# k and q in two loads of 48 rows, gates contiguous, constants in two tiles, and one activation table asked for first

## The chip, the cores and the metric

The kernel runs on one NeuronCore of a Trainium2 chip. The metric is the device time of one execution in microseconds. Three runs of the kernel before gave 475.73, 475.87 and 477.15 us; the median is 475.87 us.

The core has five engines that run side by side, each working off its own row of instructions in order: TensorE (PE; the loads of its stationary operand are shown apart as PEld), VectorE (DVE), ScalarE (ACT), GpSimd (POOL) and SyncE (SP), which here issues nearly all DMAs. An instruction starts when its engine is free and the semaphores that it waits for have been raised.

## The reference

Two batches of eight heads go through a gated recurrence over 768 time steps with head size 40 (mLSTM); the result, 1536 tokens of 320 values, goes through two gated feed-forward layers of width 1536.

```python
for t in range(S):                       # S = 768
    m_new = np.maximum(f_gate[:, :, t] + m, i_gate[:, :, t])
    f_stab = np.exp(f_gate[:, :, t] + m - m_new)
    i_stab = np.exp(i_gate[:, :, t] - m_new)
    m = m_new
    C = f_stab[:, :, None, None] * C + i_stab[:, :, None, None] * np.einsum('bhd,bhe->bhde', vt, kt)
    n = f_stab[:, :, None] * n + i_stab[:, :, None] * kt
    h_tilde = np.einsum('bhde,bhe->bhd', C, qt)
    nq = np.einsum('bhd,bhd->bh', n, qt)[:, :, None]
    y[:, :, t] = o * h_tilde / np.maximum(np.abs(nq), 1.0)     # o = sigmoid(o_gate)

x = (sigmoid(x @ w_gate) * (x @ w_val)) @ w_out                # layer 1
x = ((x @ w_a) * (x @ w_b)) @ w_out2                           # layer 2
```

Everything but the six feed-forward weights is float32; the weights arrive as float64.

## The kernel before

The recurrence is computed in 12 steps of 64 time steps each. In step s the decay between two time steps comes out of the gates: a matmul E (two of them, for even and odd heads, `ph_E`, line 366, into a tile e) makes the exponents out of the tiles lhsE and rhsE, and ScalarE exponentiates them (X, `ph_exp`, line 373, into Dt). The products of k and q are S (`ph_S`, lines 396 and 411, out of the tile kq). VectorE multiplies S by Dt (P, line 421, into Z), and k by a column of Dt (Kw, line 376). TensorE then makes the step's output O (line 440) and the state for the next step, ST (line 430), which ScalarE copies back into the tile Y (line 452). The feed-forward units (lines 519 to 528) follow as tokens become ready, and take most of the time. Two tiles are used alternately for e (two banks), Dt and Z, three for kq and Y.

The weights come as pairs of 32-bit words; ScalarE and VectorE turn each block into float32 (lines 213 to 237) and split it (lines 247 to 258). The gates are loaded in three chunks of 128, 320 and 320 time steps; their running maximum and sums are `gate_parts` (lines 276 to 307).

A constant tile cs holds, side by side, an identity matrix (for transposes, and as a stationary operand in S), the patterns for rhsE and lhsE, a small identity for Y (`y_init`, line 569) and two columns of signs for the gates.

The order of each engine's instructions is that of the written list PLAN. A task stands there by name: E10 is the matmul E of step 0, odd heads (E, then the half, then the step), X00 its exponential, kq0 a load, na0 the first conversion of weight block 0, ge1 the gate step on ScalarE. A number behind a star, as in `E00*37`, puts that many dummy matmuls on a zeroed tile in front (line 169, tile first). A DMA waits for what its destination needs and, since eight semaphores are used in turn, for the eighth DMA before it.

The kernel's first activation (line 193) writes two elements that are overwritten later; it is there for its activation table. A table has to be loaded before a function that the present one lacks; copy and absolute value need none.

Of the kernel before, what the change touches and what calls it, by code (L numbers as in the profile page):

```python
# [7 lines left out]
F32 = mybir.dt.float32  # L8
# [43 lines left out]
NH = 4 * P + DM  # L52
E1 = D + 1

C_ID = 0
C_RE = C_ID + P
C_LD = C_RE + 512
C_IP = C_LD + 2 * P
C_AB = C_IP + D
C_N = C_AB + 2  # L60


EXP_LO = 2.0**-15
# [1 line left out]


PLAN = """
start gl1 cst rhs0:A lhs0:A ga0 ga1 gb0 gd0 ge0 lhs1:A w0 gb1 na0 gc0 gd1 ge1 pr0:V E00*37 og0 X00 rhs1:A
pr1:V nb0 yz0 kv0 E01*1 E10*6 gl2 gc1 yz2 ns0 yz1 kv1 X01 X10 ga2 pr2:V yi0:A nc0 k10:V kq0 yi2:A k00:V E11*4
X11 S0 pr3:V w1 kq1 E02 kq2 nd0:V E12 P10 P00 yi1:A k01:G kv2 ST0 st0 na1 X02 og2 S1*10 X12 k11:G k12:G og1  # L70
kq3 gb2 gd2 O0 kv3 ST1 P11 P01 S2*2 pr4:V sg0 nb1 E03 s10 N0 O1*2 P02 P12 st1 s30:G k02:G kq4 ST2 sg2 N1 s20:V
# [59 lines left out]
def kernel(  # L131
    ctx: ExitStack,
    tc: tile.TileContext,
    gates: bass.AP,
    cst: bass.AP,
    kqT: bass.AP,
    kv: bass.AP,
    ogate: bass.AP,
# [4 lines left out]
    nc = tc.nc  # L143
# [34 lines left out]


    cs = xpool.tile([P, C_N], F32, tag="cs", name="cs")  # L180
    ident = cs[:, C_ID : C_ID + P]

    x2tok = xpool.tile([P, NSTEP, 3 * P], F32, tag="x2tok", name="x2tok")

# [5 lines left out]

    Y = [apool.tile([P, 2, NPAIR, B, E1 + D], F32, tag=f"Y{i}", name=f"Y{i}") for i in range(3)]
    Z = [apool.tile([P, 2, NPAIR, B, T], F32, tag=f"Z{i}", name=f"Z{i}") for i in range(2)]
    nc.scalar.activation(Z[0][:, 0, 0, 0, 0:2], zb[:, 0:2], AF.Sigmoid)
    Kw = [apool.tile([P, 2, NPAIR, B, D], F32, tag=f"Kw{i}", name=f"Kw{i}") for i in range(2)]
    PR = ((slice(64, 128), slice(0, 64)), (slice(0, 64), slice(64, 128)))

# [67 lines left out]
    def load_gates(i):  # L264

        c0, n = GCH[i]
        w = wpool.tile([P, 2 * NH + 2 * P], F32, tag=f"W{NWB - 1 - i}", name=f"gates{i}")[0:64]
        g = w[:, 0 : 2 * n].rearrange("p (x t) -> p x t", x=2)
        gws[i] = g, w[:, 2 * n : 3 * n], w[:, 3 * n : 4 * n], w[:, 4 * n : 5 * n + 1]
        nc.sync.dma_start(g, gates[:, :, c0 : c0 + n])  # L270

    def gate_parts(i):
        c0, n = GCH[i]
        s0 = 0 if i else 1

        def part0():
            g, lf, L, ms = gws[i]
            if i == 0:
                nc.vector.memset(ms[:, 0:1], -1e30)
                nc.vector.memset(lf[:, 0:1], 0.0)  # L280
            else:
                nc.vector.tensor_copy(ms[:, 0:1], mlast[0])
            nc.vector.tensor_tensor_scan(ms[:, 1:], g[:, 1], g[:, 0], ms[:, 0:1], op0=ALU.add, op1=ALU.max)
            mlast[0] = ms[:, n : n + 1]
            nc.vector.tensor_tensor(lf[:, s0:], g[:, 1, s0:], ms[:, s0:n], op=ALU.add)

        def part1():
            g, lf, L, ms = gws[i]
            nc.vector.tensor_tensor(lf[:, s0:], lf[:, s0:], ms[:, s0 + 1 :], op=ALU.subtract)
            nc.vector.tensor_tensor(g[32:64, 0], g[32:64, 0], ms[32:64, 1:], op=ALU.subtract)  # L290

        def part2():
            g, lf, L, ms = gws[i]
            nc.vector.tensor_tensor_scan(L, rm[:, 0:n], lf, 0.0, op0=ALU.mult, op1=ALU.add)
            nc.vector.tensor_tensor(L[32:64], g[32:64, 0], L[32:64], op=ALU.subtract)

        def part3():
            g, lf, L, ms = gws[i]
            hi = g[:, 1].bitcast(F32R)
            nc.scalar.activation(hi, L, AF.Copy)  # L300
            nc.scalar.activation(lf, hi.bitcast(F32), AF.Copy, scale=cs[0:64, C_AB + 1 : C_AB + 2])

        def part4():
            g, lf, L, ms = gws[i]
            nc.vector.scalar_tensor_tensor(
                V[:, c0 : c0 + n], L, cs[0:64, C_AB : C_AB + 1], lf, op0=ALU.mult, op1=ALU.subtract
            )

        return part0, part1, part2, part3, part4


# [78 lines left out]
    def ph_S(s):  # L390
        if s < NQ:

            sp = [ps_tile("acc", f"sp{par}_{s}") for par in range(2)]
            for par in range(2):
                _, qr = PR[par]
                nc.tensor.matmul(
                    sp[par][qr],
                    cs[qr.start : qr.start + D, C_ID + qr.start : C_ID + qr.stop],
                    kq[s][qr.start : qr.start + D, 1].rearrange("p a b t -> p (a b t)"),
                    start=True, stop=True,  # L400
                )
# [98 lines left out]
    def ph_T(s):  # L500
        Tps[s] = transp(ps_tile("e", f"tp{s}"), xtok[s])
# [61 lines left out]
    def y_init(i, e):  # L563
        for par in range(2):
            _, qr = PR[par]
            y = Y[i][qr, par, :, :, E1:].rearrange("p a b d -> p (a b) d")
            x = cs[qr, C_IP : C_IP + D].unsqueeze(1).to_broadcast([64, NPAIR * B, D])
            if e is None:
                nc.scalar.activation(y, x, AF.Copy)
            else:  # L570
                e.tensor_copy(y, x)
# [99 lines left out]

    task("start", "D", lambda: load_gates(0))
    task("cst", "D", lambda: nc.sync.dma_start(cs, cst))

    def t_copy(e, out, x):
        if e is None:
# [12 lines left out]
        task(f"lhs{i}", "AG", lambda e, i=i: t_lhs(i, e), ("cst",))  # L689
    for i in range(3):  # L690
        task(f"yz{i}", "G", lambda i=i: nc.gpsimd.memset(Y[i].rearrange("p x a b e -> p (x a b e)"), 0.0))
        task(f"yi{i}", "AG", lambda e, i=i: y_init(i, e), ("cst", f"yz{i}"))
    for i in range(len(OGS)):
        task(f"og{i}", "D", lambda i=i: load_og(i))
        task(f"sg{i}", "A", lambda i=i: ph_sig(i), (f"og{i}",))
# [2 lines left out]
    for i, (c0, n) in enumerate(GCH):  # L698
        if i:
            task(f"gl{i}", "D", lambda i=i: load_gates(i))  # L700
        a, b, c, c2, c3 = gate_parts(i)
        task(f"ga{i}", "V", a, [f"gl{i}" if i else "start"] + ([f"ga{i-1}"] if i else []))
        task(f"gb{i}", "V", b, [f"ga{i}"])
        task(f"gd{i}", "V", c, [f"gb{i}"])
        task(f"ge{i}", "A", c2, [f"gd{i}", "cst"])
        task(f"gc{i}", "V", c3, [f"ge{i}"])
    for i in range(NPREP // 2, NSTEP // 2):
        s = 2 * i
# [4 lines left out]
    for s in range(NSTEP):  # L713
# [16 lines left out]
                task(f"q{p}{n}", "VG", lambda e, s=s, p=p: ph_qg(s, p, e), ["kq" + n, f"X{p}{n}"] + back("O", 2))  # L730
            task(f"k{p}{n}", "VG", lambda e, s=s, p=p: ph_kw(s, p, e), ["kv" + n, f"yi{s % 3}", f"X{p}{n}"] + back("ST", 2))
        if s < NQ:
            task("S" + n, "P", lambda s=s: ph_S(s), ["kq" + n, "cst"], [("acc", [f"P{p}{n}"]) for p in range(2)])
        else:
            task("S" + n, "P", lambda s=s: ph_S(s), ["kq" + n], [("e", ["P0" + n, "P1" + n])])
        o_in = [z + n for z in zs] + ["kv" + n, f"yi{s % 3}"] + back("st", 1)
# [95 lines left out]
    assert len(done) == len(tasks)  # L832


_INS = ["gates", "cst", "kqT", "kv", "ogate", "w1", "w2"]


def _layout(inputs):
# [15 lines left out]
    def rows(g):  # L854
        return g[rb, 2 * rpair + rpar]

    a["gates"] = np.stack([rows(ig), rows(fg)], 1)

    def tr(z):

        z = z.reshape(B, NPAIR, 2, NSTEP, T, D).transpose(2, 5, 3, 1, 0, 4)
        o = np.zeros((P, NSTEP, NPAIR * B * T), dt)
        o[:D], o[64 : 64 + D] = z.reshape(2, D, NSTEP, NPAIR * B * T)
        return o.transpose(1, 0, 2)

    a["kqT"] = np.concatenate([tr(k), tr(q)], 2)
# [38 lines left out]
    for par in range(2):  # L905
# [5 lines left out]
    c[0:D, C_IP : C_AB] = np.eye(D)
    c[64 : 64 + D, C_IP : C_AB] = np.eye(D)
    lo = rlo == 1
    c[0:64, C_AB] = lo
    c[0:64, C_AB + 1] = np.where(lo, 1.0, -1.0)
# [23 lines left out]
```

## Time and profile before

| | |
|---|---|
| median of three runs | 475.87 us |
| the profiled execution | 475.26 us |
| its span, from the first to the last instruction | 473.4 us |
| TensorE busy | 463.8 us (98%) |
| VectorE busy | 295.5 us (62%) |
| ScalarE busy | 242.7 us (51%) |
| GpSimd busy | 102.5 us (22%) |
| moved by DMA | 39.31 MB, 83 GB/s over the span |

Busy time is the time in which an instruction of the engine runs. Matmuls overlap and their ends are modelled, so that a busy TensorE is not TensorE at its peak. The time stands for the whole run; single stages have other limits, so they are read in windows of time. Times in rows count from the start of the span. In a row of a timeline the first number is the start, the second the duration, and the bracket says how long the engine had stood idle before, and what, by the profile, ended that. The granted clock (PEclk) is 1.00 where TensorE's records show no throttling.

### The profile page before, as it was taken

How to read it: one execution, taken by the hardware profiler on the slowest of the kernel's cores; microseconds unless marked ns; L12 is line 12 of the kernel's file. 1: busy time of each engine (PE TensorE's matmuls, PEld its weight loads, DVE VectorE, ACT ScalarE, POOL GpSimd, SP SyncE). 2: the span in 40 equal slices, each digit the busy share in tenths (PEclk: the TensorE clock that was granted, in tenths of full speed). 3: DMA queues.
4: the chain of work that ended last, by engine and by line, in shares of the span. 5: the costliest groups of instructions: out<-in, count | busy, mean ns of one | idle time of the engine just before them, and what ended most of it. 6: DMA issues, size and time to landing. Idle time of an engine off the chain costs nothing.

```text
span 473.4 us, 8681 instructions
## 1 busy us (share of the span) xinstructions
PE 463.8 (98%) x3516; PEld 404.1 (85%) x3516; DVE 295.5 (62%) x505; ACT 242.7 (51%) x455; POOL 102.5 (22%) x110
## 2 busy tenths in 40 slices
PE   9899999999999999999999999999999999999995
PEld 3478989999998889888888898888989888888885
DVE  7989998998655663637675564565655727524243
ACT  5999978668672635343464432645452415322130
POOL 3234327613340014100320311103140003200000
PEclk9899999999999999999999999999999999999998
DMA  7968454243022040300202120024021020001121
GB/s 239 335 203 281 150 162 114 60 147 114 1 83 84 1 168 12 131 25 1 83 1 83 66 102 1 6 86 160 10 80 77 1 84 1 0 1 26 31 55 55
DMA packets 10454, 39.31 MB, mean 83 GB/s; under 512 B 1840, under 2 KB 3760, under 8 KB 10416
## 3 DMA queue, kind: packets, MB, share of 16 engines
q1 hardware_dynamic: 10128, 38.45, 25.0%
q8 instruction: 27, 0.44, 0.4%
q10 hardware_dynamic: 288, 0.33, 0.2%
q14 instruction: 11, 0.09, 0.1%
HBM read 36.71 MB, written 1.97 MB: 82 GB/s over the span
## 4 chain that ended last, share of the span: by engine, by line
PE 86%; DVE 6%; DMA 3%; ACT 2%; issue 1%; POOL 1%; DVEq 0%; POOLq 0%
PE pa L519 30%; PE pb L519 23%; PE acc L526 8%; PE acc L527 8%; PE acc L528 8%; PE o L440 2%; DMA Y<-in_kv_dram 2%; DMA kq<-in_kqT_dram 2%; PE sp L411 2%; PE st L430 1%; PE first L169 1%; PE t L482 1%; DVE g L551 1%; PE tp L482 1%; PE e L366 1%; DVE Z L421 1%
## 5 line engine op out<-in xcount | busy, mean ns | idle before, releaser
L519 PE MATMUL pa<-xb,W 128*128 128x512 f32 (+1 forms) x864 | 169.7, 344 | 0.2 <-DVE ge L600 0.2
L519 PEld LDWEIGHTS pa<-xb,W 128*128 128x128 f32 x864 | 136.4, 188 | 19.1 <-DVE ge L600 0.6
L519 PE MATMUL pb<-xb,W 128*128 128x512 f32 x480 | 119.0, 392 | 0.0
L519 PEld LDWEIGHTS pb<-xb,W 128*128 128x128 f32 x480 | 89.0, 188 | 17.9
L555 ACT ACTIVATE gh<-g 128x512 fp32r<-128x512 f32 (+1 forms) x84 | 47.5, 568 | 110.5 <-PE acc L527 55.6
L526 PE MATMUL acc<-W,gh 128*128 128x320 f32 x288 | 89.3, 310 | 0.0
L527 PE MATMUL acc<-W,gh 128*128 128x320 f32 x288 | 88.9, 309 | 0.0
L528 PE MATMUL acc<-W,gl 128*128 128x320 f32 x288 | 88.8, 308 | 0.0
L549 DVE TENSOR_TENSOR g<-g,pb 128x512 f32<-128x512 f32 x60 | 40.9, 685 | 69.7 <-PE pb L519 61.7
L560 DVE TENSOR_TENSOR gl<-g,gh 128x512 fp32r<-128x512 f32 (+1 forms) x66 | 45.5, 694 | 44.0 <-ACT gh L555 43.9
L544 ACT ACTIVATE g<-pa 128x512 f32<-128x512 f32 x60 | 35.6, 595 | 45.8 <-DVE gl L560 38.1
L527 PEld LDWEIGHTS acc<-W,gh 128*128 128x128 f32 x288 | 54.0, 188 | 2.1
L526 PEld LDWEIGHTS acc<-W,gh 128*128 128x128 f32 x288 | 54.0, 188 | 2.0
L528 PEld LDWEIGHTS acc<-W,gl 128*128 128x128 f32 x288 | 54.0, 188 | 0.0
L253 POOL TENSOR_TENSOR W<-wst,W 128x832 fp32r<-128x832 f32 x9 | 19.1, 2123 | 84.5 <-DVE x2tok L634 42.2
L634 DVE SCALAR_TENSOR_TENSOR x2tok<-acc,x2tok 128x320 f32<-128x320 f32 x52 | 23.8, 484 | 19.5 <-PE acc L528 19.5
L237 POOL TENSOR_TENSOR wst<-cva,wst 128x960 int32<-128x960 int32 x7 | 16.9, 2411 | 73.9 <-DVE cva L231 61.1
L213 ACT ACTIVATE cva<-wst 128x960 f32<-128x960 f32 x24 | 25.8, 1075 | 10.4 <-DVE wst L237 8.8
L247 ACT ACTIVATE W<-wst 128x832 fp32r<-128x832 f32 x24 | 23.1, 965 | 12.0 <-DVE wst L237 9.0
L231 DVE SCALAR_TENSOR_TENSOR cva<-wst,cva 128x960 int32<-128x960 int32 x24 | 27.9, 1160 | 0.4
L560 POOL TENSOR_TENSOR gl<-g,gh 128x256 fp32r<-128x256 f32 x18 | 15.7, 877 | 54.6 <-ACT gh L555 44.9
L214 ACT ACTIVATE wst<-wst 128x960 int32<-128x960 uint32 x24 | 25.9, 1080 | 0.0
(85 smaller groups left out, 473.1 us busy)
## 6 DMA issues: line engine op xcount, KB each, us to landing
wst<-in_w_dram SPq DMA_DIRECT2D x24, 960.0 KB
kq<-in_kqT_dram SPq DMA_DIRECT2D x12, 512.0 KB
Y<-in_kv_dram SPq DMA_DIRECT2D x24, 162.0 KB
out_dram<-x2tok SPq DMA_DIRECT2D x10, 160.0 KB
og<-in_ogate_dram SPq DMA_DIRECT2D x1, 960.0 KB
og<-in_ogate_dram SPq DMA_DIRECT2D x1, 640.0 KB
cs<-in_cst_dram SPq DMA_DIRECT2D x1, 469.0 KB
rhsE<-V SPq DMA_DIRECT2D x24, 2.0 KB
```

The source lines that it names most:

```text
L213: nc.scalar.activation(cva[0], hi.bitcast(F32), AF.Abs)
L214: nc.scalar.activation(lo, lo.bitcast(U32), AF.Copy, scale=2.0**-29)
L231: nc.vector.scalar_tensor_tensor(ai, hi, -0x40000000, ai, op0=ALU.bitwise_and, op1=ALU.bitwise_or)
L519: nc.tensor.matmul(dst, w[:, w0 : w0 + P], x[:, h, cb], start=(i == 0), stop=(i == 7))
L526: nc.tensor.matmul(a, gh[:, c], wh, start=st, stop=False)
L527: nc.tensor.matmul(a, gh[:, c], wl, start=False, stop=False)
L528: nc.tensor.matmul(a, gl[:, c], wh, start=False, stop=sp)
L544: nc.scalar.activation(t, pa, AF.Copy if l else AF.Sigmoid)
L549: nc.vector.tensor_tensor(t, t, pb, op=ALU.mult)
L555: nc.scalar.activation(gh, g, AF.Copy)
L560: eng.tensor_tensor(gl, g, gh.bitcast(F32), op=ALU.subtract)
L634: nc.vector.scalar_tensor_tensor(dst[:, 0:DM], acc, half, dst[:, 0:DM], op0=ALU.mult, op1=ALU.add)
```

## The change

- kqT holds 48 rows for each half of the heads (40 and 8 of zeros) instead of 128 rows in all, and `load_kq` issues two DMAs, into partitions 0 to 47 and 64 to 111.
- The gates lie chunk by chunk in memory, each row of a chunk contiguous, and the two columns of signs lie in front of the first chunk; that chunk has a tile of its own, g0.
- The two identities move out of cs into a tile ci, loaded by a DMA of its own behind cs. cs shrinks from 938 columns to 768; ci has 176.
- The first activation is an exponential instead of a sigmoid.

```diff
-C_ID = 0
-C_RE = C_ID + P
+C_RE = 0
 C_LD = C_RE + 512
-C_IP = C_LD + 2 * P
-C_AB = C_IP + D
-C_N = C_AB + 2
+C_N = C_LD + 2 * P
+I_ID = 0
+I_IP = I_ID + P
+I_N = I_IP + D + 8
@@ PLAN
-start gl1 cst rhs0:A lhs0:A ga0 ...
+start gl1 cst cid rhs0:A lhs0:A ga0 ...
@@ tile_mlstm_moe_kernel
+    g0 = g0pool.tile([64, 2 + 2 * GCH[0][1]], F32, tag="g0", name="g0")
+    sel, sign = g0[:, 0:1], g0[:, 1:2]
 ...
-    ident = cs[:, C_ID : C_ID + P]
+    ci = xpool.tile([P, I_N], F32, tag="ci", name="ci")
+    ident = ci[:, I_ID : I_ID + P]
 ...
-    nc.scalar.activation(Z[0][:, 0, 0, 0, 0:2], zb[:, 0:2], AF.Sigmoid)
+    nc.scalar.activation(Z[0][:, 0, 0, 0, 0:2], zb[:, 0:2], AF.Exp)
@@ load_gates
-        g = w[:, 0 : 2 * n].rearrange("p (x t) -> p x t", x=2)
+        g = (w if i else g0[:, 2:])[:, 0 : 2 * n].rearrange("p (x t) -> p x t", x=2)
-        nc.sync.dma_start(g, gates[:, :, c0 : c0 + n])
+        if i:
+            nc.sync.dma_start(w[:, 0 : 2 * n], gates[:, 2 + 2 * c0 : 2 + 2 * (c0 + n)])
+        else:
+            nc.sync.dma_start(g0, gates[:, 0 : 2 + 2 * n])
@@ gate_parts
-            nc.scalar.activation(lf, hi.bitcast(F32), AF.Copy, scale=cs[0:64, C_AB + 1 : C_AB + 2])
+            nc.scalar.activation(lf, hi.bitcast(F32), AF.Copy, scale=sign)
-                V[:, c0 : c0 + n], L, cs[0:64, C_AB : C_AB + 1], lf, op0=ALU.mult, op1=ALU.subtract
+                V[:, c0 : c0 + n], L, sel, lf, op0=ALU.mult, op1=ALU.subtract
@@ load_kq
-        nc.sync.dma_start(kq[s].rearrange("p x a b t -> p (x a b t)"), kqT[s])
+        x = kq[s].rearrange("p x a b t -> p (x a b t)")
+        for h in range(2):
+            nc.sync.dma_start(x[64 * h : 64 * h + KR], kqT[s, h])
@@ ph_S and y_init: cs[..., C_ID ...] and cs[qr, C_IP ...] become
+                    ci[qr.start : qr.start + D, I_ID + qr.start : I_ID + qr.stop],
+            x = ci[qr, I_IP : I_IP + D].unsqueeze(1).to_broadcast([64, NPAIR * B, D])
@@ tasks
     task("cst", "D", lambda: nc.sync.dma_start(cs, cst))
+    task("cid", "D", lambda: nc.sync.dma_start(ci, cid))
```

ScalarE's row of instructions around the first exponentials, before: cva0 and wst0 are the conversion of the first weight block, Dt0_0 is X00's result, Y0 and Y2 are two of the three tiles Y.

```order
L213 ACTIVATE cva0_130<-wst0_126 128x960
L214 ACTIVATE wst0_126<-wst0_126 128x960
L300 ACTIVATE gates1_107<-gates1_107 64x320
L301 ACTIVATE gates1_107<-gates1_107,cs_87 64x320
L373 ACT_TABLE_LOAD
L373 ACTIVATE Dt0_0_181<-e0_0_177 128x512
L677 ACTIVATE rhsE1_91<-cs_87 128x1024
L373 ACTIVATE Dt0_1_209<-e0_1_191 128x512
L373 ACTIVATE Dt1_0_211<-e1_0_199 128x512
L569 ACTIVATE Y0_94<-cs_87 64x8x40 x2
L569 ACTIVATE Y2_96<-cs_87 64x8x40 x2
L373 ACTIVATE Dt1_1_233<-e1_1_231 128x512
```

The same place of the same row in the changed kernel:

```order
L219 ACTIVATE cva0_136<-wst0_132 128x960
L220 ACTIVATE wst0_132<-wst0_132 128x960
L309 ACTIVATE gates1_112<-gates1_112 64x320
L310 ACTIVATE gates1_112<-gates1_112,g0_85 64x320
L384 ACTIVATE Dt0_0_187<-e0_0_183 128x512
L689 ACTIVATE rhsE1_96<-cs_91 128x1024
L384 ACTIVATE Dt0_1_215<-e0_1_197 128x512
L384 ACTIVATE Dt1_0_217<-e1_0_205 128x512
L580 ACTIVATE Y0_99<-ci_92 64x8x40 x2
L580 ACTIVATE Y2_101<-ci_92 64x8x40 x2
L384 ACTIVATE Dt1_1_240<-e1_1_238 128x512
```

The table load in front of the first exponential is gone; the order is the same otherwise, and the copies into Y read ci.

SP's row of DMAs from the third load of gates on, before, with the semaphores that each waits for (DMAHW0 to DMAHW7 are the eight of the DMAs; wst1 is the second weight block, og the output gate):

```order
L270 DMA gates2_201<-in_gates_dram 64x2x320
L319 DMA Y1_95<-in_kv_dram 64x648 [waits DMAHW0_49,Pool_49]
L320 DMA Y1_95<-in_kv_dram 64x648 [waits DMAHW1_49]
L315 DMA kq0_222<-in_kqT_dram 128x1024 [waits DMAHW2_49]
L206 DMA wst1_257<-in_w1_dram 128x1920 [waits DMAHW3_49]
L315 DMA kq1_259<-in_kqT_dram 128x1024 [waits DMAHW4_49]
L315 DMA kq2_263<-in_kqT_dram 128x1024 [waits DMAHW5_49]
L319 DMA Y2_96<-in_kv_dram 64x648 [waits DMAHW6_49]
```

The same place in the changed kernel:

```order
L277 DMA gates2_207<-in_gates_dram 64x640 [waits DMAHW0_49]
L330 DMA Y1_100<-in_kv_dram 64x648 [waits DMAHW1_49,Pool_49]
L331 DMA Y1_100<-in_kv_dram 64x648 [waits DMAHW2_49]
L326 DMA kq0_228<-in_kqT_dram 48x1024 [waits DMAHW3_49]
L326 DMA kq0_228<-in_kqT_dram 48x1024 [waits DMAHW4_49]
L212 DMA wst1_264<-in_w1_dram 128x1920 [waits DMAHW5_49]
L326 DMA kq1_266<-in_kqT_dram 48x1024 [waits DMAHW6_49]
L326 DMA kq1_266<-in_kqT_dram 48x1024 [waits DMAHW7_49]
L326 DMA kq2_271<-in_kqT_dram 48x1024 [waits DMAHW0_49]
L326 DMA kq2_271<-in_kqT_dram 48x1024 [waits DMAHW1_49]
L330 DMA Y2_101<-in_kv_dram 64x648 [waits DMAHW2_49]
```

ci's DMA stands earlier, behind that of cs, so all semaphores are one further; kq0's second half waits for DMAHW4, the first weights, where kq0 as a whole waited for DMAHW2, cs. wst1 waits for the first load of og where it had waited for the first weights.

## Rows read from the trace of the kernel before

**Rows 1.** The page, part 4: the chain that ended last.
```profile
PE 86%; DVE 6%; DMA 3%; ACT 2%; issue 1%; POOL 1%; DVEq 0%; POOLq 0%
```

**Rows 2.** Windows: stretch, length, busy PE, PEld, DVE, ACT, POOL, clock, DMA share, GB/s.
```profile
0.00:25.00 25.00, 21.93 (x156) 10.35 (x158) 20.04 (x43) 18.14 (x29) 5.97 (x9) 0.93 0.92 293
98.00:473.00 375.00, 369.90 (x2195) 328.01 (x2193) 208.76 (x335) 162.65 (x294) 64.14 (x66) 1.00 0.16 54
```

**Rows 3.** Timeline of TensorE: start us, us, engine line operation.
```profile
15.02 0.50 PE L366 MATMUL e<-rhsE,lhsE 128*128 128x512 f32 x1 [1.22 <-ACT Dt L373]
...
16.89 0.65 PE L396 MATMUL sp<-kq,cs 40*64 40x512 f32 x2
...
18.25 0.50 PE L366 MATMUL e<-rhsE,lhsE 128*128 128x512 f32 x1
19.38 0.50 PE L366 MATMUL e<-rhsE,lhsE 128*128 128x512 f32 x1 [0.63 <-DMA kq<-in_kqT_dram]
19.81 1.32 PE L430 MATMUL st<-Y,Kw 128*40 128x41 f32 x32
21.07 3.40 PE L169 MATMUL first<-zb 128*128 128x512 bf16 x10
...
33.60 0.65 PE L396 MATMUL sp<-kq,cs 40*64 40x512 f32 x2
```

**Rows 4.** Timeline of ScalarE.
```profile
10.04 1.09 ACT L213 ACTIVATE cva<-wst 128x960 f32<-128x960 f32 x1 [1.47 <-DMA wst<-in_w_dram]
...
13.08 1.28 ACT L373 ACT_TABLE_LOAD   x1
14.37 0.60 ACT L373 ACTIVATE Dt<-e 128x512 f32<-128x512 f32 x1
...
18.73 0.60 ACT L373 ACTIVATE Dt<-e 128x512 f32<-128x512 f32 x1
...
21.18 0.90 ACT L452 ACTIVATE Y<-st 40x328 f32<-40x328 f32 x2 [0.86 <-PE st L430]
...
29.70 2.97 ACT L334 ACTIVATE x2tok<-og 128x1920 f32<-128x1920 f32 x2
```

**Rows 5.** Timeline of VectorE.
```profile
15.95 0.68 DVE L340 TENSOR_TENSOR rhsE<-V,cs 32x512 fp32r<-32x512 f32 x1 [0.25 <-ACT rhsE L677]
...
18.03 0.89 DVE L376 TENSOR_TENSOR Kw<-Y,Dt 128x320 f32<-128x320 f32 x2
```

**Rows 6.** Longest waits by engine from 21 (others 22) to 67 us: us, times, longest.
```profile
PE tp L482 <- ACT Dt L373: 0.2, 1, 0.2
ACT W L247 <- DVE wst L237: 1.1, 3, 0.5
DVE Z L421 <- PE sp L411: 1.4, 1, 1.4
```

**Rows 7.** Windows of time up to 30 us, columns as in rows 2.
```profile
0.00:10.00 10.00, 8.83 (x30) 3.56 (x31) 6.60 (x20) 4.28 (x7) 3.60 (x7) 1.00 0.74 232
10.00:16.00 6.00, 4.78 (x22) 2.07 (x21) 5.13 (x11) 5.90 (x8) 0.00 (x0) 1.00 1.05 312
16.00:18.00 2.00, 1.95 (x38) 1.21 (x36) 1.96 (x3) 1.96 (x5) 0.00 (x0) 1.00 1.00 410
18.00:22.00 4.00, 3.37 (x40) 2.11 (x40) 3.96 (x8) 3.05 (x7) 2.10 (x2) 0.73 1.06 294
22.00:28.00 6.00, 6.00 (x115) 3.77 (x113) 4.46 (x9) 5.92 (x8) 1.02 (x2) 0.90 0.75 291
28.00:30.00 2.00, 2.00 (x40) 1.47 (x39) 1.97 (x7) 1.91 (x6) 1.32 (x3) 1.00 0.62 166
20.00:25.00 5.00, 5.00 (x66) 2.76 (x66) 4.40 (x7) 4.08 (x7) 2.28 (x2) 0.67 1.02 338
```

**Rows 8.** Timeline of SP: the issue of kq0.
```profile
7.31 0.58 SPq L315 DMA_DIRECT2D kq<-in_kqT_dram  x1
```

**Rows 9.** Waits of VectorE up to 30 us: us in total, times, longest.
```profile
DVE gates L283 <- DMA gates<-in_gates_dram: 2.2, 2, 1.5
```

More of the change, by code (lines that the diff above doesn't have):

```diff
@@ L46 @@
 NPREP = 6
+KR = 48
 OGS = ((0, 2, 3), (2, 6, 3), (6, 12, 4))
@@ L67 @@
 PLAN = """
-start gl1 cst rhs0:A lhs0:A ga0 ga1 gb0 gd0 ge0 lhs1:A w0 gb1 na0 gc0 gd1 ge1 pr0:V E00*37 og0 X00 rhs1:A
+start gl1 cst cid rhs0:A lhs0:A ga0 ga1 gb0 gd0 ge0 lhs1:A w0 gb1 na0 gc0 gd1 ge1 pr0:V E00*37 og0 X00 rhs1:A
 pr1:V nb0 yz0 kv0 E01*1 E10*6 gl2 gc1 yz2 ns0 yz1 kv1 X01 X10 ga2 pr2:V yi0:A nc0 k10:V kq0 yi2:A k00:V E11*4
@@ L135 @@
     cst: bass.AP,
+    cid: bass.AP,
     kqT: bass.AP,
@@ L154 @@
     gpool = ctx.enter_context(tc.tile_pool(name="gpool", bufs=1))
+    g0pool = ctx.enter_context(tc.tile_pool(name="g0pool", bufs=1))
+    g0 = g0pool.tile([64, 2 + 2 * GCH[0][1]], F32, tag="g0", name="g0")
+    sel, sign = g0[:, 0:1], g0[:, 1:2]
     slots = {}
@@ L397, in ph_S @@
                     sp[par][qr],
-                    cs[qr.start : qr.start + D, C_ID + qr.start : C_ID + qr.stop],
+                    ci[qr.start : qr.start + D, I_ID + qr.start : I_ID + qr.stop],
                     kq[s][qr.start : qr.start + D, 1].rearrange("p a b t -> p (a b t)"),
@@ L566, in y_init @@
             y = Y[i][qr, par, :, :, E1:].rearrange("p a b d -> p (a b) d")
-            x = cs[qr, C_IP : C_IP + D].unsqueeze(1).to_broadcast([64, NPAIR * B, D])
+            x = ci[qr, I_IP : I_IP + D].unsqueeze(1).to_broadcast([64, NPAIR * B, D])
             if e is None:
@@ L691 @@
         task(f"yz{i}", "G", lambda i=i: nc.gpsimd.memset(Y[i].rearrange("p x a b e -> p (x a b e)"), 0.0))
-        task(f"yi{i}", "AG", lambda e, i=i: y_init(i, e), ("cst", f"yz{i}"))
+        task(f"yi{i}", "AG", lambda e, i=i: y_init(i, e), ("cid", f"yz{i}"))
     for i in range(len(OGS)):
@@ L704 @@
         task(f"gd{i}", "V", c, [f"gb{i}"])
-        task(f"ge{i}", "A", c2, [f"gd{i}", "cst"])
+        task(f"ge{i}", "A", c2, [f"gd{i}"])
         task(f"gc{i}", "V", c3, [f"ge{i}"])
@@ L732 @@
         if s < NQ:
-            task("S" + n, "P", lambda s=s: ph_S(s), ["kq" + n, "cst"], [("acc", [f"P{p}{n}"]) for p in range(2)])
+            task("S" + n, "P", lambda s=s: ph_S(s), ["kq" + n, "cid"], [("acc", [f"P{p}{n}"]) for p in range(2)])
         else:
@@ L743 @@
         task("D" + n, "A", lambda s=s: ph_twice(s), ["M" + n])
-        task("T" + n, "P", lambda s=s: ph_T(s), ["D" + n, "cst"], [("e", ["xl" + n])])
+        task("T" + n, "P", lambda s=s: ph_T(s), ["D" + n, "cid"], [("e", ["xl" + n])])
         task("xh" + n, "A", lambda s=s: ph_xh(s), ["T" + n])
@@ L832 @@
     assert len(done) == len(tasks)
-_INS = ["gates", "cst", "kqT", "kv", "ogate", "w1", "w2"]
+_INS = ["gates", "cst", "cid", "kqT", "kv", "ogate", "w1", "w2"]
 def _layout(inputs):
@@ L855, in rows @@
         return g[rb, 2 * rpair + rpar]
-    a["gates"] = np.stack([rows(ig), rows(fg)], 1)
+    g = np.stack([rows(ig), rows(fg)], 1)
+    lo = rlo == 1
+    ab = np.stack([lo, np.where(lo, 1.0, -1.0)], 1).astype(g.dtype)
+    a["gates"] = np.concatenate([ab] + [g[:, :, c : c + n].reshape(64, 2 * n) for c, n in GCH], 1)
     def tr(z):
         z = z.reshape(B, NPAIR, 2, NSTEP, T, D).transpose(2, 5, 3, 1, 0, 4)
[L862 to L866, printed above, removed]
+        o = np.zeros((NSTEP, 2, KR, NPAIR * B * T), dt)
+        o[:, :, :D] = z.reshape(2, D, NSTEP, NPAIR * B * T).transpose(2, 0, 1, 3)
+        return o
+    a["kqT"] = np.concatenate([tr(k), tr(q)], 3)
     def tok(z):
@@ L894, in _layout @@
     a["w2"] = pack(inputs["moe2_w_a"], inputs["moe2_w_b"], inputs["moe2_w_out"])
-    c = np.zeros((P, C_N), f32)
-    c[:, C_ID : C_ID + P] = np.eye(P)
+    c, c2 = np.zeros((P, C_N), f32), np.zeros((P, I_N), f32)
+    c2[:, I_ID : I_ID + P] = np.eye(P)
     blk = np.zeros((64, NPAIR, B, T), f32)
@@ L910, in _layout @@
         d[64:, tk] = np.eye(64)
[L911 to L915, printed above, removed]
+    for r in (0, 64):
+        c2[r : r + D, I_IP : I_IP + D] = np.eye(D)
+    a["cid"] = c2
     a["cst"] = c
```

## The prediction

> **What bounds the kernel now.** I read the page's chain of waits first: it is 86% TensorE [rows 1]. Then busy time by stage: from 98 us on TensorE is busy for 369.9 of 375 us and nothing in the edits touches that work, so only its start can move. In the first 25 us TensorE is busy for 21.93 us [rows 2]: the holes are there, 3.07 us. So I read the first 25 us in order of time, engine by engine.
>
> TensorE stands 1.22 us before the matmul at 15.02 us, for ScalarE's exponential, and 0.63 us before the one at 19.38 us, whose row names a kq transfer [rows 3]. The second name I do not believe: that matmul reads rhsE and lhsE, not kq, and writes a bank that ScalarE's exponential at 18.73 us (0.60 us long) has emptied; it starts 0.05 us after that ends [rows 3, 4]. So both waits lead to ScalarE. Its row from 10.04 us, when the first weights have landed (1.47 us of waiting for them), has no named wait until 21.18 us: conversion of weights, two gate steps, a table load of 1.28 us at 13.08 us, the exponential at 14.37 us, a copy into rhsE, two exponentials, four copies into Y, the exponential at 18.73 us [rows 4].
>
> **The table load.** The dummy activation at the start now asks for the exponential's table, so its load at 0.72 us stays under the wait for constants, and the load at 13.08 us goes, since all between are copies and absolute values. From its start to that of the exponential behind it are 1.29 us [rows 4]: this much leaves ScalarE's row.
>
> [...]
>
> What is late next, step by step. The exponential starts at 13.08 and ends at 13.68 us. TensorE's dummies before its next matmul end at 13.80 (15.02 - 1.22), so that matmul starts at 13.8: 1.2 us. The copy, the exponentials and the copies into Y each follow directly and move by 1.29, so the matmul at 19.38 moves to 18.1. The state product ST0 behind it, at 19.81 us, is then held by VectorE instead: it reads the Kw tiles written from 18.03 to 18.92 us. VectorE stands only 0.25 us before that, for rhsE at 15.95 us, so Kw is ready at 18.67 and ST0 starts at 18.7: 1.1 us [rows 3, 5]. ScalarE had waited 0.86 us for ST0 at 21.18 [rows 4] and moves by the same 1.1.
>
> Does it last? Between 21 and 67 us TensorE waits 0.2 us in all; ScalarE's longest sum is 1.1 us, for VectorE; VectorE's is 1.4 us, for TensorE [rows 6]. That last one lets VectorE, ahead by only 0.25 us, catch up: 0.25 + 1.4 = 1.65, more than 1.1. The three rows then move together, and the matmul stage begins 1.1 us earlier.
>
> **The dummies at half clock.** [...] I take 0.1.
>
> **The halves of kq.** Each load of 512 KB on 128 rows becomes two of 48 rows, 384 KB together (0.393 MB). The trace has no such transfer; bounds from the nearest stretches [rows 7]. Whole-height loads, 16 to 18 us: 410 GB/s, so 1.28 us for the old load and 0.96 for the new bytes, a gain of 0.32. Mostly 64-row halves of Y, 28 to 30 us: 166 GB/s, 2.37 us, a loss of 1.09. A mixed queue, 18 to 22 us: 294 GB/s, 1.34 us, a loss of 0.06. I take the last, since the new halves stand in just such a queue, so nearly zero, and keep both ends.
>
> [...]
>
> What hides it. Bytes ahead of and with kq0 are 3.37 MB. 2.32 MB had moved by 10 us (232 GB/s), the rest at 312 GB/s takes until 13.4 us. A load is complete later than that mean: the first weights (1.69 MB with what is ahead) were complete at 10.04, 0.63 MB or 2.0 us late [rows 4, 7]. So kq0 is there near 15.4 us. It is read at 16.89 us; after the change it is wanted at 15.6, and may come until 16.3 without moving the matmul at 18.1 (less 1.36 for its own products and 0.44 for one matmul between) [rows 3]. In the same way the 960 KB of ogate (6.72 MB) are there at 25.8, read within ScalarE's row at 29.70, and kq3 (7.90 MB) at 29.9, read at 33.60 [rows 3, 4, 7]. After the change the last two are wanted at 28.5 and 32.4: over 2 us to spare if a load costs nothing more.
>
> **The queue's waits.** Each load waits for the eighth before it, and there are more loads now: kq0, issued at 7.31 us [rows 8], goes out in two, and the second half waits for the first weights, 10.04 us; behind it in SP's row stand the second weights, kq1, kq2 and Y. By 10 us 2.32 MB had moved, and the list up to kq0's first half is 3.0 MB, so 0.7 MB or 2.2 us of work is still ahead; the queue does not run dry. An extra issue costs SP about the 0.58 us of that row, beside a full queue. Cost zero; where it did run dry, the upper end above stands for it.
>
> **Constants and gates.** The copies into rhsE and lhsE wait for 384 KB instead of 469, perhaps 0.3 us less, and then ScalarE still waits for weights that have the same bytes ahead of them and one more issue. Contiguous gates may shorten VectorE's 2.2 us of waiting for them [rows 9], but TensorE works off its 37 dummies first, whatever VectorE does, and ScalarE's row hangs on the weights. I take zero, between a gain of 0.3 and a loss of 0.6 (one issue).
>
> **Sum.** 1.1 + 0.1 + 0 + 0 + 0 = 1.2 us off the profiled execution's 475.26 us (a span of 473.4 and 1.9 around it): 474.1. The median of the runs, 475.87, stands 0.6 above it, so I predict 475.87 - 1.2 = 474.7. What a measurement of this kernel can tell from no change is about 0.3%, 1.4 us: the forecast lies just inside.
>
> **Rivals.**
> [...]
> 2. Slower: the halves run at their lower end. With 1.09 us more for each of kq0 to kq3, kq3 is there at 34.3 and S3, wanted at 32.4, is 1.9 us late; -1.2 + 1.9 = +0.7: 476.6. It decides from 0.63 us per load on ((32.4 - 29.9) / 4). [...] Against it: in a full queue halves overlap with whole loads, as 294 shows, and the stretch of 166 was not always full.
> [...]
> 4. The weights land 1.2 us later behind the extra small load; ScalarE's row starts that much later and the table's gain is gone: 475.9. Against it: the bytes ahead are the same.
>
> **Chances.** Forecast 0.54 (474.2 to 475.4), rival 1 0.20, rival 2 0.13, rival 3 0.08, rival 4 0.05. The range for 8 in 10 is 473.3 to 476.2. Faster by over 0.3% (under 474.4): 0.4 of the forecast's share and nearly all of rival 1's, 0.39. Slower (over 477.3): the far part of rivals 2 and 3, 0.07. Between: 0.54.
>
> **What would show it.** Right: no load near 13 us on ScalarE and its first exponential there; no hole before the matmul now at 15.02; ST0 near 18.7 us, the product S1 behind the ten dummies near 23.2 instead of 24.4, S3 near 32.4, and the same shift at 100 us. Rival 2: TensorE waiting at S for kq, or ScalarE for ogate. [...] Wrong: a shift at ST0 that is gone at 100 us.

## The result and the profile after

Forecast: 474.7 us. Measured: a median of 477.63 us against 475.07 for the kernel before, 20 runs each; the ratio is 1.0060 with a 95% interval of 1.0041 to 1.0079. The change is slower by about 2.9 us where 1.2 less was expected, and above the range. The profiled execution took 477.32 us, its span 475.5.

ScalarE's timeline of the changed kernel shows the first half of the story:

```profile
12.19 1.07 ACT L219 ACTIVATE cva<-wst 128x960 f32<-128x960 f32 x1 [3.27 <-DMA wst<-in_w_dram]
...
15.09 0.57 ACT L384 ACTIVATE Dt<-e 128x512 f32<-128x512 f32 x1
...
21.67 0.90 ACT L463 ACTIVATE Y<-st 40x328 f32<-40x328 f32 x2 [0.65 <-PE st L441]
```

The table load is gone: from the first weights to the first exponential it is 2.90 us, where it was 4.33 [rows 4]. But the weights came at 12.19 instead of 10.04, so the row ends up later, not earlier.

TensorE's timeline of the changed kernel, to be laid beside [rows 3]:

```profile
15.72 0.50 PE L377 MATMUL e<-rhsE,lhsE 128*128 128x512 f32 x1 [1.55 <-ACT Dt L384]
...
20.81 0.81 PE L441 MATMUL st<-Y,Kw 128*40 128x41 f32 x32 [0.24 <-issue]
21.56 2.33 PE L174 MATMUL first<-zb 128*128 128x512 bf16 x10
24.47 1.24 PE L407 MATMUL sp<-kq,ci 40*64 40x512 f32 x3 [0.57 <-DVE Z L432]
...
27.26 0.56 PE L441 MATMUL st<-Y,Kw 128*40 128x41 f32 x19
28.94 0.43 PE L441 MATMUL st<-Y,Kw 128*40 128x41 f32 x13 [1.13 <-issue]
...
34.41 0.37 PE L451 MATMUL o<-Y,Z 128*64 128x41 f32 x5
35.20 1.01 PE L451 MATMUL o<-Y,Z 128*64 128x41 f32 x27 [0.42 <-issue]
36.14 0.65 PE L407 MATMUL sp<-kq,ci 40*64 40x512 f32 x2
...
42.27 0.47 PE L441 MATMUL st<-Y,Kw 128*40 128x41 f32 x14 [0.73 <-issue]
```

S1 starts at 24.47, nearly where it stood before; S3 starts at 36.14 instead of 33.60. In between and behind it are three holes in the middle of rows of equal matmuls, 1.13, 0.42 and 0.73 us, 2.28 in all, and none of them ends on a named wait. No matmul's wait names a kq tile here; two weight loads of S do, 0.9 us in all, beside a busy TensorE. Windows of the same kernel, columns as in [rows 2], to be laid beside [rows 7]:

```profile
10.00:16.00 6.00, 3.78 (x15) 1.41 (x13) 3.65 (x8) 3.77 (x6) 0.00 (x0) 1.00 0.92 183
18.00:22.00 4.00, 3.76 (x72) 2.33 (x71) 3.94 (x7) 3.24 (x7) 1.40 (x2) 1.00 1.02 237
20.00:25.00 5.00, 4.19 (x46) 1.99 (x45) 4.96 (x8) 3.00 (x7) 1.88 (x2) 1.00 1.06 223
```

The DMA engines are as busy as before (shares of 0.92 to 1.06) and move far less: 183 instead of 312 GB/s, 237 instead of 294, 223 instead of 338. The granted clock from 20 to 25 us is 1.00 instead of 0.67 (in the kernel before 0.50 from 20 to 23 us and 0.87 from 23 to 24: a piece at half clock), and the ten dummies take 2.33 instead of 3.40 us; S1 then stands 0.57 us for VectorE's Z, so nothing of that is left either. The piece is no fixed part of the kernel before: a second profile of it, e15 below, has 0.50 from 20 to 25 us.

Does the shift last? The chain of each kernel has a piece that can be set side by side, 64 matmuls of a later S, in the kernel before and then in the changed one:

```profile
114.76 2.01 PE sp L411 x64
```
```profile
116.99 2.01 PE sp L422 x64
```

2.23 us there, and 2.1 in the spans. At S3 it was 2.54. TensorE's waits from 14 to 70 us (us in total, times, longest) say what was added and what gave a part back; the kernel before, then the changed one:

```profile
PE st L430 <- DVE Kw L376: 0.8, 1, 0.8
```
```profile
PE st L441 <- issue: 2.1, 3, 1.1
...
PE o L451 <- issue: 0.4, 1, 0.4
```

The wait for Kw is gone, as TensorE now comes later; the issue waits, the three holes and 0.24 us at ST0, are new.

### The profile page after: what moved, and what is told of

It reads as the page before. It is cut to its first block, busy times and chain, and to the rows that moved or that the text cites. A ratio compares the mean times of both kernels' runs of the same rounds, so it can differ in the third digit from the quotient of the medians.

```text
span 475.5 us, 8698 instructions
## 1 busy us (share of the span) xinstructions
PE 463.1 (97%) x3516; PEld 403.3 (85%) x3516; DVE 295.1 (62%) x505; ACT 241.3 (51%) x454; POOL 101.9 (21%) x110
## 4 chain that ended last, share of the span: by engine, by line
PE 90%; DVE 3%; DMA 2%; SPq 1%; ACT 1%; issue 1%
PE pa L530 31%; PE pb L530 23%; PE acc L537 9%; PE acc L538 9%; PE acc L539 9%; PE o L451 2%; PE sp L422 2%; DMA wst<-in_w_dram 2%; PE st L441 1%; PE e L377 1%; PE t L493 1%; PE tp L493 1%; SPq L370 1%; DVE wst L243 1%; PE sp L407 0%
```

## The experiments

All against the kernel before on the same chip; ratios of device times with 95% intervals, 6 to 12 runs each (e15 is one run).

**One part at a time (e1 to e4).** Theory A held that the loss starts in the head of the queue, rival B that the halves carry it.

e1, the table alone:
```
-    nc.scalar.activation(Z[0][:, 0, 0, 0, 0:2], zb[:, 0:2], AF.Sigmoid)
+    nc.scalar.activation(Z[0][:, 0, 0, 0, 0:2], zb[:, 0:2], AF.Exp)
```


> The kernel before with the exponential's table asked for first, and nothing else of the change. Both theories: the term of the prediction holds by itself, so 1.0 to 1.5 us faster than before, no load at 13 us, first weights at 10.0 us on ScalarE as before, ST0 near 18.7 us. If the term itself were wrong: within 0.4 us of before.

Measured 0.9979 (0.9946 to 1.0011): not told from no change. The load is gone, but in its profile the first weights came at 12.31 us, with a queue that is word for word that of before.

e2, the halves alone (kqT laid out as 12 x 2 x 48 rows):
```
+        for h in range(2):
+            nc.sync.dma_start(x[64 * h : 64 * h + KR], kqT[s, h])
```


> The kernel before with kq in two loads of 48 rows alone. Theory A (the loss starts in the head, before any kq moves, by the gates' or the constants' new loads): first weights at 10.0 us as before, 0 to 1 us slower than before. [...]

Measured 1.0062 (1.0032 to 1.0092), 2.95 us: as much as the whole change, so rival B by its time (2.5 to 4 us for the halves), and by the rate from 14 to 22 us, 240 GB/s (it had under 250). The waits for kq, Kw or weights that it looked for are not there. Its TensorE:

```profile
25.86 0.56 PE L433 MATMUL st<-Y,Kw 128*40 128x41 f32 x19
28.79 0.43 PE L433 MATMUL st<-Y,Kw 128*40 128x41 f32 x13 [2.37 <-issue]
```

The same place, a hole of 2.37 us. Behind it the clock falls: 0.50 from 30 to 35 us, over real work.

```profile
30.00:35.00 5.00, 4.98 (x57) 3.42 (x57) 1.29 (x2) 1.97 (x2) 1.45 (x3) 0.50 0.67 115
```

So the same loss is paid in another way. The changed kernel's profile has holes and a clock of 1.00 from 20 to 40 us. Over the runs behind the ratios the median granted clock is 0.995 in the changed kernel and 0.995 to 0.997 in the kernel before, but 0.988 in e2. A difference of 0.008 over a run of 476 us is 3.8 us of work at full clock (an estimate): in e2 the clock can account for most or all of the loss, in the changed kernel for little of it. e8 (0.989) and e11 (0.991) below are like e2.

e3, the gates contiguous and the two sign columns in front of them:
```
+            nc.sync.dma_start(g0, gates[:, 0 : 2 + 2 * n])
```


> The kernel before with the gates contiguous by chunk and the signs in front, alone. Theory A in the form that the gates' loads clog the queue (64 rows of 2560 B, at rows of 6152 B, where there were 128 pieces of 1280 B): first weights on ScalarE at 11.5 to 12.2 us, 1.5 to 2.5 us slower than before. Rival B: first weights at 10.0 us, within 0.5 us of before.

Measured 1.0001 (0.9968 to 1.0034): nothing, as B had it.

e4, the constants in two tiles and loads (the signs stay in cs):
```
+    ci = xpool.tile([P, I_N], F32, tag="ci", name="ci")
+    task("cid", "D", lambda: nc.sync.dma_start(ci, cid))
```


> The kernel before with the constants in two tiles and two loads, alone. Theory A in the form that the extra load in front of the weights delays them: first weights on ScalarE at 11.5 to 12.2 us, 1.5 to 2.5 us slower than before. Rival B and theory A in its other form: first weights at 10.0 to 10.4 us, within 0.5 us of before.

Measured 1.0119 (1.0068 to 1.0169), 5.7 us, more than the whole change and against both theories. e13 settles it below.

**Where the halves cost (e5 to e8).** e5 is the changed kernel with kq whole:
```
-        for h in range(2):
-            nc.sync.dma_start(x[64 * h : 64 * h + KR], kqT[s, h])
+        nc.sync.dma_start(kq[s].rearrange("p x a b t -> p (x a b t)"), kqT[s])
```


> The changed kernel with kq loaded whole again (table, gates and constants stay). Theory A (the halves carry the loss: 2.9 us alone): 1 us faster than before to equal, 474.5 to 476 against 476, no piece at half clock before 30 us, kq1 landed by 21 us. Theory B (the second constants' load carries a loss of its own, 5.7 us alone): still 2 to 5 us slower than before, with the third exponent matmul or ST0 over 1.5 us later than before.

Measured 1.0001 (0.9973 to 1.0028): theory A. Its first weights came at 12.26 us, as late as in the changed kernel, so late weights do not part the two profiles; the kernels differ in the halves alone. e5 has no hole in ST1, and S3 starts at 34.52 instead of 36.14.

e6, table and gates together (both edits above):
```
+    nc.scalar.activation(Z[0][:, 0, 0, 0, 0:2], zb[:, 0:2], AF.Exp)
+            nc.sync.dma_start(g0, gates[:, 0 : 2 + 2 * n])
```


> Before with the exponentials' table first and the contiguous gates, and nothing else. Theory A (the gains of parts add): 0.8 to 1.3 us faster than before, no table load near 13 us. Theory B (the table's gain was the spread of runs): within 0.5 us of before, with ST0 no earlier than 19.8 us because the first weights land at 11 to 12.3 us.

Measured 0.9994 (0.9967 to 1.0020): theory B; weights at 11.35.

e7, halves from kq4 on:
```
+        if s < 4:
+            nc.sync.dma_start(x, kqT[s])
+        else:
+            for h in range(2):
+                nc.sync.dma_start(x[64 * h : 64 * h + 48], kqT[s, 64 * h : 64 * h + 48])
```


> Before with kq0 to kq3 loaded whole and kq4 on in two parts of 48 rows. Theory A (halves cost in the full queue of the first 35 us): within 0.5 us of before. Theory B (a half costs wherever it stands, through VectorE's and GpSimd's reads or the queue's waits): 1.5 to 3 us slower, with TensorE waiting at a later S or O.

Measured 0.9996 (0.9965 to 1.0026): the loss is that of the first four loads.

e8, halves of 64 rows:
```
+        for h in range(2):
+            nc.sync.dma_start(x[64 * h : 64 * h + 64], kqT[s, 64 * h : 64 * h + 64])
```


> Before with each kq in two loads of 64 rows, so the old 512 KB. Theory A (the price is that of a transfer on one half of the rows, by bytes): a third more bytes than with 48 rows, so a third more loss, 3.5 to 4.5 us slower than before. Theory B (the price is the second issue and its place in the queue of eight): 2.5 to 3 us slower, as with 48 rows.

Measured 1.0110 (1.0076 to 1.0143), 5.2 us. The interval is 3.6 to 6.8 us: theory A's 3.5 to 4.5 overlaps it, theory B's 2.5 to 3 does not; but the intervals of e2 and e8 overlap, so what the bytes saved with 48 rows are worth is not shown. Its weights came at 9.91, as early as ever, and it still has the hole, at the 20th matmul of ST1. Late weights are not its cause.

```profile
24.95 0.56 PE L432 MATMUL st<-Y,Kw 128*40 128x41 f32 x19
27.59 0.46 PE L432 MATMUL st<-Y,Kw 128*40 128x41 f32 x13 [2.08 <-issue]
```

**What the hole is (e9, e10).** e9 puts six dummies more in front of the first E of the changed kernel:
```
-... ge1 pr0:V E00*37 og0 ...
+... ge1 pr0:V E00*43 og0 ...
```


> The changed kernel with 43 dummies instead of 37 ahead of the first matmul E, so every later instruction of TensorE stands 12 places further on in its program (a dummy is a weight load and a matmul). Theory A (the hole of 1.13 us in the middle of ST1 is a wait for the next piece of TensorE's program, which comes by DMA behind the loads): the hole stays at the same place of the program, so ST1 is cut 6 matmuls earlier, 13 ahead of the hole instead of 19. Theory B (ST1 waits for a tile of kq, Y or Kw that lands late): the cut stays behind the 19th matmul. The time tells nothing between them: within 1 us of the changed kernel, 1.5 to 3.5 us above before.

Measured 1.0051 (1.0014 to 1.0087). TensorE's timeline:

```profile
27.39 0.44 PE L441 MATMUL st<-Y,Kw 128*40 128x41 f32 x13
28.78 0.58 PE L441 MATMUL st<-Y,Kw 128*40 128x41 f32 x19 [0.95 <-issue]
```

13 matmuls ahead of the hole instead of 19. The hole belongs to a place in TensorE's program, not to a tile. Counting the matmuls of the timelines from the start says the same: the changed kernel's three holes stand behind matmul 219, 344 and 469, 125 apart, e9's again behind 219, and those of e7, e10 and e12 behind 220 and 345. TensorE is free there, and no row names a semaphore that it waits for: the two conditions for a start that stand at the head of the document do not account for the 1.13 us. My reading is that TensorE has run out of instructions. No row says so; the page's DMA part has queues of kind "instruction", the larger of them, in the changed kernel (the kernel before has the same line):

```profile
q8 instruction: 27, 0.44, 0.4%
```

TensorE has 3516 matmuls and as many weight loads; over 27 packets that is 260 a packet (an estimate), about the 250 of both kinds between two holes. So I take q8 for TensorE's queue.

The DMA view of half a microsecond shows when the first of those packets moves (queue, kind: packets, MB, share). In the kernel before, from 24 to 24.5 us:

```profile
q1 hardware_dynamic: 44, 0.21, 103.3%
q8 instruction: 1, 0.02, 13.7%
```

In e5, from 24.5 to 25 us:

```profile
q8 instruction: 1, 0.02, 14.5%
```

In the changed kernel, from 26.5 to 27 us:

```profile
q1 hardware_dynamic: 27, 0.17, 81.6%
q8 instruction: 1, 0.02, 14.1%
```

ST1 of the kernel before and of e5:

```profile
26.70 0.79 PE L430 MATMUL st<-Y,Kw 128*40 128x41 f32 x32
```
```profile
27.17 0.79 PE L439 MATMUL st<-Y,Kw 128*40 128x41 f32 x32
```

The 32 matmuls go out in 0.73 us, so TensorE is at the 20th near 27.1, 27.5 and, in the changed kernel, 27.6 us. It goes on at once, at once, and at 28.94. Read packet by packet in the traces, this first packet starts at 24.07, 24.99 and 26.51 us and takes 1.1, so it has landed at 25.17, 26.15 and 27.64. All twenty profiles keep to one pattern. In fifteen of them TensorE stops inside ST1, a later O or ST2 up to 45 us, twenty times in all, and each time it goes on 1.23 to 1.62 us after the packet has landed. In the five without such a hole (the kernel before, e4, e5, e14, e15) the packet has landed 1.38 to 2.70 us ahead of TensorE.

What makes the packet too late is its time against TensorE's. In e8 it starts at 24.82, no later than in e5, but TensorE is at the place at 25.3 and stands. Nor does the first packet part the cut by rows from the rest: e1, e3, e6, e7, e10, e13, e16, e17 and e18, whose first four loads of kq span all rows, have one hole of 0.2 to 1.1 us in ST1 as well, and none of them is measurably slower than before. This is e18, the whole change with kq cut by columns (below), which loses nothing:

```profile
26.54 0.56 PE L441 MATMUL st<-Y,Kw 128*40 128x41 f32 x19
28.14 0.43 PE L441 MATMUL st<-Y,Kw 128*40 128x41 f32 x13 [1.04 <-issue]
```

The second packet parts them better. It starts at 27.3 to 31.9 us in the thirteen profiles with kq loaded over all rows, and at 32.3 to 34.9 in those with rows left out or cut (the changed kernel, e2, e8, e11, e12, and e7 with halves from kq4 on; e9, with halves too, is out of line at 30.5). The changed kernel has three holes. That these stops, and the clock behind the longest of them, make up the loss is shown for single executions only: e5 and the changed kernel differ by 1.62 us at S3, where the two holes before it are 1.55. How often the other executions stop is not on record.

e10 adds a load of 590 KB that nobody reads to the kernel before:
```
+    task("ox", "D", lambda: nc.sync.dma_start(xo, ogate[:, 0:1152]))     # behind og1, ahead of kq3
```


> Before with one load more, 128 rows of 4.6 KB (590 KB) into a tile that nobody reads, behind the two large loads of ogate and ahead of kq3. Theory A (a fuller queue makes TensorE's program late): a hole that ends on no named wait inside ST1, 0.5 to 2 us, though kq0 to kq2 and ogate land as before; 0.5 to 2.5 us slower. Theory B (only a tile that lands late costs): kq3 lands 1.8 us later, near 31, still ahead of its reader at 33.6; no hole in ST1, within 0.5 us of before.

Measured 0.9978 (0.9940 to 1.0016). Theory A fell on the time: the profile has the holes (1.12 us in ST1, 1.63 in a later O), yet the runs are no slower. In that execution S1 stood at 22.86 us, 1.5 earlier than before, with the clock at 1.00 from 20 to 25 us; the holes ate this lead and more: it took 476.92 us, where the median of e10 is 475.22. e7's profile is like it: holes of 0.39 and 1.36 us, 477.64 us against a median of 475.08. So the holes seem to cost in the execution that has them, and to differ from one execution to the next. This longer queue alone is no measurable harm.

**Height or number of loads (e11, e14).** e11 loads rows 0 to 111 in one piece, e14 all 128 rows in two pieces by columns:
```
+        nc.sync.dma_start(x[0:112], kqT[s, 0:112])                                                     # e11
+        for h in range(2):                                                                             # e14
+            nc.sync.dma_start(x[:, 512 * h : 512 * h + 512], kqT[s, :, 512 * h : 512 * h + 512])       # e14
```


> Before with each kq in one load of the rows 0 to 111 (458 KB instead of 524). Theory A (the price is that of a transfer on one half of the rows): no loss, between 0.7 us faster and 0.3 slower. Theory B (any load that is not of all 128 rows is slow): 1 to 3 us slower, and the loads of kq take longer per byte as with halves.

> Before with each kq in two loads of all 128 rows and half the columns (2 KB a row), so the old 524 KB and as many issues as with halves of rows. Theory A (the price is that of a load that is not of full height): within 0.7 us of before, kq2 landed by 23 us, no hole in ST1 longer than 0.8 us. Theory B (the price is the second issue and its waits in the queue of eight): 2 to 3 us slower, as with 48 rows, and kq2 near 25 us.

e11: 1.0043 (1.0003 to 1.0083), slower, with a hole of 2.22 us: theory B, though it is a single load with 66 KB less, and just clear of the noise; e12 below, with the same 112 rows, loses too. e14: 0.9960 (0.9936 to 0.9985), faster by 1.9 us, with as many issues as the halves by rows and no hole in ST1. So in these runs neither the number of loads nor the bytes set the price, but whether a load spans all 128 rows. Why such loads are slow stays open. The loads' queue from 14 to 22 us in the kernel before, in the changed one, in e5, in e11 and in e14:

```profile
q1 hardware_dynamic: 661, 2.79, 102.7%
```
```profile
q1 hardware_dynamic: 472, 1.93, 94.7%
```
```profile
q1 hardware_dynamic: 672, 2.73, 104.5%
```
```profile
q1 hardware_dynamic: 509, 2.10, 102.2%
```
```profile
q1 hardware_dynamic: 977, 2.83, 105.3%
```

Bytes by engine time (share x 16 engines x 8 us): 21.2 GB/s per engine before, 15.9 changed, 20.4 in e5, 16.1 in e11, 21.0 in e14. The two kernels with loads of fewer than 128 rows have the low rates.

**The constants again (e13).** As e4, with the second tile narrower:
```
-I_N = I_IP + D + 8
+I_N = I_IP + D
```


> Before with the constants in two tiles and two loads, as in e4, but the second tile 8 columns narrower, so that every tile behind them keeps the address that it has before (in e4 they moved by 32 bytes). Theory A (e4's loss came largely from the moved addresses: its matmuls pa and pb took 396 and 395 ns instead of 393 and 392, 960 of them): 393 and 392 ns again, and between 0.5 us faster and 1.5 slower than before. Theory B (the second load itself costs): still 4 to 6 us slower.

Measured 1.0022 (0.9995 to 1.0048): theory A. The groups by line of e4 and then of e13, from 100 us on:

```profile
L522 PE MATMUL pa<-xb,W 128*128 128x512 f32 x480 | 121.1, 396 | 0.0
L522 PE MATMUL pb<-xb,W 128*128 128x512 f32 x480 | 120.7, 395 | 0.0
```
```profile
L522 PE MATMUL pa<-xb,W 128*128 128x512 f32 x480 | 119.5, 393 | 0.0
L522 PE MATMUL pb<-xb,W 128*128 128x512 f32 x480 | 119.1, 392 | 0.0
```

3.2 us on those two rows. e4's loss was largely that of my version of the edit, which pushed later tiles by 32 bytes; the change as made has 393 and 392.

**The spread of the first weights (e15).** The kernel before, unchanged:


> The kernel before, unchanged, profiled once more. If the landing of the first weights varies by itself: anywhere between 9.9 and 12.3 us (10.04 in the first profile), and the time follows it by less than half, 473 to 478. If it is fixed by the program: 10.0 us again, and no hole in ST1.

477.04 us. Its ScalarE and TensorE:

```profile
12.20 1.06 ACT L213 ACTIVATE cva<-wst 128x960 f32<-128x960 f32 x1 [2.71 <-DMA wst<-in_w_dram]
```
```profile
17.16 0.50 PE L366 MATMUL e<-rhsE,lhsE 128*128 128x512 f32 x1 [2.69 <-ACT Dt L373]
```

2.16 us later than in the first profile, with the same program. Over the eleven profiles whose first loads are those of before the weights came between 9.32 and 12.31 us, median 10.10; over the six with the extra small load between 11.32 and 12.30, median 12.06. That the small load delays them is likely, and not shown by so few. In time it does not show: e13, with the small load, is at 1.0022 and e5 at 1.0001.

**Better orders (e12, e16 to e18).** e12 is table, gates and 112 rows; e16 is the table with kq3 ahead of the two large ogate loads; e17 the table with halves by columns; e18 the whole change with halves by columns:
```
-... yi1:A k01:G kv2 ST0 st0 na1 X02 og2 S1*10 X12 k11:G k12:G og1 kq3 gb2 ...
+... yi1:A k01:G kv2 ST0 st0 na1 X02 kq3 og2 S1*10 X12 k11:G k12:G og1 gb2 ...       # e16
```


> Before with the exponentials' table first, the contiguous gates, and each kq in one load of 112 rows: what is left of the change without its two costly parts. If the parts add: 0.5 to 1.8 us faster than before. If the spread in the landing of the first weights hides them: within 0.5 us of before.

> Before with the exponentials' table first, and kq3 loaded ahead of the two large loads of ogate (4 KB packets where 7.7 KB packets stand when TensorE asks for the next piece of its program). Theory A (the piece comes behind a fixed number of packets): it lands 0.5 to 1 us earlier than with the table alone, no hole in ST1 over 0.4 us, 0.5 to 2 us faster than before. Theory B (ogate is then late for ScalarE, 30 us instead of 29.7): within 0.7 us of before or slower.

> Before with the exponentials' table first and each kq in two loads of all rows and half the columns. Theory A (the two parts add): 2 to 3.2 us faster than before. Theory B (the table's 1.3 us on ScalarE is taken back by a later wait): 1.3 to 2 us faster, as with the columns alone.

> The whole change, with kq cut by columns (two loads of all 128 rows, 524 KB) instead of rows. Theory A (the cut by rows is the only step that turned the forecast round): 0.5 to 3 us faster than before. Theory B (the second constants' load and the weights landing at 12 us eat the gain): within 0.7 us of before.

e12: 1.0062 (1.0025 to 1.0099); 112 rows lose here too. e16: 0.9987 (0.9958 to 1.0016), theory B by its time, but not by its reason: ScalarE's two large copies of ogate start at 28.62 us, with no named wait, and the hole in ST1 is 0.21 us, as theory A had it. e17: 0.9961 (0.9934 to 0.9988), theory B: the table adds nothing that can be measured to e14. e18: 1.0011 (0.9981 to 1.0040), theory B: cut by columns the change loses nothing and gains nothing. e14 and e17 beat the kernel before by 0.4%, and so the changed one too. Why e14 is faster than whole loads, which move as many bytes as fast, is open.

## Why the prediction was wrong

**The failed step is "The halves of kq", with "What hides it".** It had two faults. The rate: 294 GB/s was taken from a mixed queue; from 14 to 22 us the changed kernel moved 241 (1.93 MB in 8 us), e5 with whole kq 341. At those rates new 0.393 MB take 1.63 us and old 0.524 MB 1.54: a loss of 0.09 us a load, close to the 0.06 of the step. What the step missed is that the loads among the halves go at the same pace: in these 8 us the changed kernel moved 0.80 MB less than e5, where three halved loads save 0.39. And the readers: the step asked when kq and ogate are read, and found over 2 us to spare. In the changed kernel's profile no matmul's wait names kq, and no wait names ogate. The step left out one user of the DMA engines, the queue of kind "instruction" (27 packets, 0.44 MB), taken here for that of TensorE's program; it has no tile, no row in the code and no named wait. The profile before held a hint, this queue in its DMA part. In place of a cost of zero the runs show 2.95 us for the halves alone (e2) and none with kq whole (e5) or cut by columns (e18); the profiles show it as stops of TensorE, 2.28 us in the changed kernel, and in e2, e8 and e11 as half clock (0.50 from 30 to 35 us) behind stops of 2.37, 2.08 and 2.22 us.

**The table load: right, and not worth what it said.** ScalarE's row became 1.43 us shorter (1.29 forecast). ST0, forecast at 18.7, came at 20.81: 18.7 plus the 2.15 us by which the weights were later. The step took 10.04 us as a property of the program; e15 shows 12.20 for the same one. With e1, e6 and e17 the gain itself cannot be told from zero.

**The dummies at half clock: too little.** No run shows the sum's term of 0.1 us. The runs showed a clock of 1.00 from 20 to 25 us in the changed kernel, so the piece at half clock went altogether; VectorE held S1 back by 0.57 us, so it gave nothing in this execution. At 0.67 and 0.50 from 20 to 25 us in two profiles of the kernel before, it was no fixed term to add.

**The queue's waits: right, as far as is shown.** e18 has as many issues and the same order as the change, and loses nothing; e14 has as many as e2, and is faster than before.

**Constants and gates: near zero, not shown to be zero** (e3 1.0001, e13 1.0022, e5 with all three other parts 1.0001). e18 differs from e17 in these two parts alone, and its median is 1.6 us higher (475.90 against 474.31, same chip), more than the 0.6 us that the prediction allowed; which of the two costs it is open.

**The rivals.** Rival 2 had the sign and slow halves (0.13), but 0.7 us of loss, and at the wrong place: no wait for kq3 is what the profile shows. Rival 4 (0.05) is what the profile shows at 12.19 us, and deserved more. The chances of rivals 1 (0.20) and 3 (0.08) are chances on the clock: that the piece from 20 to 25 us goes, with a gain, or that one more comes, with a loss. It went (1.00), without the gain; one more shows in e2, e8 and e11 (0.50 from 30 to 35 us), behind the holes and not behind waits for ScalarE or VectorE.

## What to carry to other kernels

Cut a load by columns, not by rows: here, in a full queue from 14 to 22 us, loads below 128 rows cost a quarter of the mean rate per engine (15.9 GB/s with 48 rows and 16.1 with 112, against 21.2 with 128 and 21.0 by columns), even with a quarter less to move; later, from kq4 on, halves cost nothing that shows (e7, 0.9996). Look at the queue of kind "instruction" too (its first packet started at 24.07 us before and at 26.51 in the changed kernel), and ask of a hole that ends on "issue" inside a row of equal matmuls whether it is a wait for it; shifting the program by a few instructions tells (e9: 13 matmuls ahead of the hole instead of 19). A landing time, a hole or a half-clock piece from one profile is one draw: profile the kernel before twice before building a sum on it.

## What was not expected of the hardware

- TensorE stopped inside a run of equal matmuls for up to 2.60 us (e12) with no named wait; the stop moved 6 matmuls ahead with 12 more instructions in front (e9), stops of one run stood 125 matmuls apart, and each ended 1.23 to 1.62 us after a packet of the instruction queue had landed. That its next instructions were late is my reading.
- With loads of 112 rows (e11) the queue was as slow per engine as with halves (16.1 against 15.9 GB/s from 14 to 22 us; 21.2 with 128 rows).
- With the tiles moved by 32 bytes (e4) 960 matmuls of 128x512 took 3 ns longer each (396 and 395 against 393 and 392 ns in e13).
- The first weights of one program landed at 10.04 us in one profile and at 12.20 in another; over eleven profiles with the same first loads, anywhere from 9.3 to 12.3.
